# Attention and top-k expert layer on one core: score and AV rounds on 64x64 tiles of TensorE

## The chip, the cores and the metric

The kernel runs on one core of one Trainium2 chip. The metric is the device time of one execution in microseconds (us), the median of several runs. Everything below about time comes from those runs or from one profiled execution.

## What is computed

The input has 8 batches, 12 heads, 448 positions and a head size of 64. First comes attention with normalised q and k, then a layer of 8 experts, each of which takes at most 80 of the 3584 tokens, those with the highest gate weight.

```python
def rmsnorm(x, g):
    rms = np.sqrt(np.mean(x * x, axis=-1, keepdims=True) + 1e-06)
    return x / rms * g
q_n, k_n = (rmsnorm(q, g_q), rmsnorm(k, g_k))
scores = scale * np.matmul(q_n, k_n.transpose(0, 1, 3, 2))
attn = softmax(scores)
x = np.matmul(attn, v)            # -> (3584, 768)
logits = x @ w_gate
expert_idx = np.argmax(logits, axis=1)
gate_w = softmax(logits)[arange(N), expert_idx]
for e in range(E):
    tok_idx = ...                 # tokens of e; over capacity: the 80 of largest gate_w
    h = np.maximum(x[tok_idx] @ w1[e], 0.0)
    out[tok_idx] = gate_w[tok_idx, None] * (h @ w2[e])
```

## The kernel before

**Groups, rounds and slots.** The work of attention is cut into 24 groups (`NG`): a batch has three, of four heads each. The four heads are two pairs, `u` = 0 and 1, and the heads of a pair are `hh` = 0 and 1. A group has seven rounds (`RD`). The loop at the end of the attention part (from L828) goes through slots -10 to 88; in each slot it issues the scores of two rounds (`S2`), the presums and AV of the two rounds before (`A2`), and what tables `begins`, `mid` and `end` have put in that slot. `mid` stands between the scores and AV, `end` behind AV. `NS` = 84 slots have scores, 0 to 83. Instructions stand on each engine in the order in which this loop issues them.

**Layout.** Of the 448 positions, 384 lie on all 128 partitions, three to a partition (`NJ`), and the last 64 (`SR`) on half of them, one pair of heads on each half. So a group has two kinds of rounds. A full round (`score`, L322) takes one pair and 128 keys: two matmuls with 64 rows (the head size) and 128 columns of the array. The round `x == NJ` (L315) takes the last 64 keys of both pairs: four matmuls of 64x64. AV (`av`) mirrors this: L344 with 128 rows (keys) and 64 columns, L337 with 64x64. All are fp32 with 448 moving columns, and each matmul stands in the trace as two instructions.

**Around the rounds.** `load` brings q, k and v into SBUF from SP's queue. `square` (ACT), `rstd` (DVE reduction, then a power on POOL), and `normalise` (POOL; DVE for groups 0 and 1) prepare q and k; `transp` transposes them on TensorE into `tp`, and ACT copies them to `qkT`. The scores land in PSUM (`ps`, two buffers), ACT writes their exponentials to `at` (L324), and DVE adds these up over the rounds (`presum`). When a pair is through, ACT copies its sum over v from PSUM (`uevac`, L367). `xout` transposes that, copies it to `xb` (one buffer) and writes it to HBM, where the experts' tokens are gathered later.

**Gate.** `zl` (L377, L381) multiplies the presums with a selector and the AV sums with the gate's weights, eight matmuls of 32 columns a group, into one PSUM bank of a batch. Then `gate1` (copy), `gate1t` (transposes), `gate1v` (reciprocal and products on DVE), `gate2`, `gate2x`, `gate2b` yield each token's expert and weight. The batches below `NB0` = 4 go through a top-k on DVE in small steps (`rounds`, `numbers`), which `work` hands out by a budget of us a slot. Each later batch is ranked in itself (`rank_in_batch`) and merged into the kept lists (`merge`, five steps); `chain_step` issues one step when its lag is over, twice a slot. What is left is issued behind the last slots, at `s == NS + 2`. The last batch is ranked after the loop (from L870). Then come gathers of tokens and the experts' matmuls (`xpose`, L962 and below).

Of the kernel before, what the change touches and what calls it, by code (L numbers as in the profile page):

```python
# [20 lines left out]
def kernel(  # L21
# [13 lines left out]
    nc = tc.nc  # L35
# [10 lines left out]
    SM = 384  # L46
# [4 lines left out]
    NB = 4 * NJ + 2  # L51
    RD = 2 * NJ + 1
# [12 lines left out]
    NB0 = 4  # L65
# [24 lines left out]

    zsel = cpool.tile([128, NQ, 32], F32, name="zsel")
    nc.vector.memset(zsel[:, :, :], 0.0)
    for i in range(NQ):
        nc.vector.memset(zsel[:, i, 24 + i:25 + i], 1.0)
    wgs = cpool.tile([128, H, 32], F32, name="wgs")
    nc.vector.memset(wgs[:, :, :], 0.0)
    wg_v = moe_w_gate.rearrange("(i c hh d) e -> hh d i c e", hh=2, c=2, d=D)

    def load_wgs():
        for hh in range(2):  # L100
            for i in range(NQ):
                nc.sync.dma_start(
                    out=wgs[hh * D:(hh + 1) * D, 4 * i + hh:4 * i + hh + 3:2, 8 * i:8 * i + 8],
                    in_=wg_v[hh, :, i])
# [12 lines left out]
    for g in range(NB0):  # L117
        nc.gpsimd.memset(offq[32 * g:32 * g + 32, :], float(g * S))
# [18 lines left out]
    nc.gpsimd.iota(rowI[:, 0:NJ], pattern=[[1, NJ]], base=0, channel_multiplier=NJ)  # L137
    nc.gpsimd.iota(rowI[:, NJ:NJ + 1], pattern=[[0, 1]], base=SM, channel_multiplier=1)
# [45 lines left out]
    tpps = ctx.enter_context(tc.tile_pool(name="tp_ps", bufs=1, space=PSUM))  # L184
    zlps = ctx.enter_context(tc.tile_pool(name="zl_ps", bufs=1, space=PSUM))
# [6 lines left out]
    with tc.tile_pool(name="vp", bufs=3) as vpool, \  # L192
         tc.tile_pool(name="attn", bufs=5) as apool, \
# [9 lines left out]
        def load(g, t, src, eng, parts=(0, 1, 2)):  # L203


            b, i = divmod(g, NQ)
            if 0 in parts:
                h0, h1 = (0, 4) if 1 in parts else (0, 2)
            elif 1 in parts:
                h0, h1 = (2, 4)  # L210
            if 0 in parts or 1 in parts:
                eng.dma_start(
                    out=t[:, h0 * NJ:h1 * NJ, :].rearrange("p (h j) d -> p h (j d)", j=NJ),
                    in_=src[b, 4 * i + h0:4 * i + h1, 0:SM].rearrange(
                        "h (p j) d -> p h (j d)", j=NJ))
            if 2 in parts:
                for u in range(2):
                    eng.dma_start(
                        out=t[64 * u:64 * u + 64, 4 * NJ:NB, :],
                        in_=src[b, 4 * i + 2 * u:4 * i + 2 * u + 2, SM:S].rearrange(  # L220
                            "h p d -> p h d"))

        def load_qk(g):
            qk = [qkpool.tile([128, NB, D], F32, tag="qk", name="qk") for _ in range(2)]
            st[g]["qk"] = qk
            if g:
                load(g, qk[0], q, nc.sync)
                load(g, qk[1], k, nc.sync)
            else:
                load(g, qk[0], q, nc.sync, (0, 2))  # L230
                load(g, qk[1], k, nc.scalar, (0, 2))
                load(g, qk[0], q, nc.sync, (1, ))
                load(g, qk[1], k, nc.sync, (1, ))
# [7 lines left out]
        M = 4 * NJ  # L241
        ALLB, HALF = [(0, NB)], ([(0, M // 2), (M, NB)], [(M // 2, M)])

# [7 lines left out]
        def rstd(g, a, parts=ALLB):  # L251
# [8 lines left out]
            for lo, hi in parts:  # L260
                if parts is HALF[0]:
# [6 lines left out]
        def normalise(g, a, parts=ALLB):  # L268
# [3 lines left out]
            eng = nc.vector if g < 2 else nc.gpsimd  # L272
            for lo, hi in parts:
                h0, h1 = lo // NJ, min(hi, M) // NJ
                if h0 < h1:
                    eng.tensor_mul(  # L276
                        qn[:, :M].rearrange("p (j h) d -> p h j d", h=4)[:, h0:h1],
                        qk[:, h0 * NJ:h1 * NJ].rearrange("p (h j) d -> p h j d", j=NJ),
                        rs[:, h0 * NJ:h1 * NJ].rearrange("p (h j) -> p h j", j=NJ)
                        .unsqueeze(3).to_broadcast([128, h1 - h0, NJ, D]))  # L280
                if hi > M:
                    eng.tensor_mul(qn[:, M:], qk[:, M:],
                                   rs[:, M:].unsqueeze(2).to_broadcast([128, 2, D]))

        def transp(g, a, u):
            tp = tpps.tile([128, 512], F32, tag="tp", name="tp")
            qn = st[g]["qn%d" % a]
            for j in range(NJ):
                nc.tensor.transpose(  # L289
                    tp[:, j * 128:(j + 1) * 128],  # L290
                    qn[:, 4 * j + 2 * u:4 * j + 2 * u + 2].rearrange("p h d -> p (h d)"),
                    ident[:, :])
            if u == 0:
                nc.tensor.transpose(tp[:, SM:512],  # L294
                                    qn[:, 4 * NJ:].rearrange("p h d -> p (h d)"), ident[:, :])
                st[g]["T%d" % a] = qktpool.tile([128, 2, S], F32, tag=f"qkT{a}", name="qkT")
            dst = st[g]["T%d" % a]
            parts = [(dst[:, 0, :], tp[:, :S]), (dst[:, 1, SM:], tp[:, S:512])] if u == 0 else \
                [(dst[:, 1, :SM], tp[:, :SM])]
            for o, x in parts:  # L300
                if a == 0:
                    nc.scalar.activation(o, x, AF.Copy, scale=gqk[:, :])  # L302
                else:
                    nc.scalar.copy(o, x)  # L304

        def score(r):
# [3 lines left out]
            if x == NJ:  # L310
                at = apool.tile([128, 2, S], F32, tag="ar", name="ar", bufs=2)
                for u in range(2):
# [740 lines left out]
```

## Time and profile before

| what | us |
|---|---|
| median of 3 runs (lowest, highest) | 532.16 (531.81, 535.04) |
| the profiled execution's own time | 529.9 |
| its span, first to last instruction | 528.2 |

The profile gives, for each engine, when it was busy: PE is TensorE (PEld its weight loads), DVE is VectorE, ACT is ScalarE, POOL is GpSimd, SP issues transfers. A matmul's end is modelled, and matmuls on different tiles overlap, so what a block of them costs is read from the start of one block to the start of the next.

### The profile page before, as it was taken

To read this page: it belongs to the slowest core of one execution; us is meant where nothing else is said; L and a number is where in the kernel's file an instruction comes from. 1 tells how busy PE (TensorE), PEld (TensorE's weight loads), DVE (VectorE), ACT (ScalarE), POOL (GpSimd) and SP (SyncE) were. 2 spreads that over 40 slices of the span, in tenths; PEclk is the share of its full clock that TensorE was granted. 3 is DMA by queue.
4 is the path that set the end of the run, shared out by engine and by line. 5 is a ranking of instruction groups with operands and counts; after the bars stand their busy time and mean duration, and the time that the engine had idled before them with its cause. 6 is when DMAs were issued, how large, how long until landed. Compare 5 with 4: busy or idle time off the path is not lost. (4 is left out here: it accounts for less than half of the span.)

```text
span 528.2 us, 9134 instructions
## 1 busy us (share of the span) xinstructions
PE 495.6 (94%) x3384; PEld 229.2 (43%) x3384; DVE 334.6 (63%) x584; ACT 315.5 (60%) x527; POOL 289.9 (55%) x212
## 2 busy tenths in 40 slices
PE   7599999999999999999999999999999989869595
PEld 7133334333433343334433333334445444568464
DVE  4575365765765658638889969996648555624242
ACT  4576786767767786678676876776666635201100
POOL 3588395883875837828467388474796000121231
PEclk9999999999999999999999999999999989668979
DMA  6469978797969995997789787969495661749931
GB/s 174 116 130 225 246 204 139 216 228 198 222 136 232 221 232 99 228 251 197 134 228 210 208 136 196 252 199 215 140 185 130 128 238 37 238 113 414 366 111 57
DMA packets 107340, 100.74 MB, mean 191 GB/s; under 512 B 28960, under 2 KB 99104, under 8 KB 106016
## 3 DMA queue, kind: packets, MB, share of 16 engines
q1 hardware_dynamic: 90736, 70.76, 45.2%
q0 software_dynamic: 16000, 29.14, 31.4%
q8 instruction: 27, 0.44, 0.4%
q10 hardware_dynamic: 560, 0.26, 0.2%
q14 instruction: 17, 0.14, 0.1%
HBM read 101.12 MB, written 39.91 MB: 267 GB/s over the span
## 5 line engine op out<-in xcount | busy, mean ns | idle before, releaser
L265 POOL TENSOR_TENSOR rs<-ms,nhalf 128x14 f32<-128x14 f32 (+1 forms) x48 | 145.7, 3039 | 130.6 <-DVE ms L258 125.7
L324 ACT ACTIVATE at<-ps 128x896 f32<-128x896 f32 x144 | 125.7, 915 | 32.7 <-PE ps L322 18.9
L322 PE MATMUL ps<-qkT 64*128 64x448 f32 x576 | 131.2, 567 | 0.6 <-ACT qkT L304 0.6
L344 PE MATMUL po<-at,vt 128*64 128x448 f32 x576 | 128.6, 561 | 0.0
L257 DVE TENSOR_REDUCE ms<-sq 128x14 f32<-128x896 f32 (+2 forms) x52 | 52.5, 1010 | 62.6 <-ACT sq L248 62.4
L356 DVE TENSOR_TENSOR sm<-at 128x896 f32<-128x896 f32 x48 | 58.7, 1224 | 26.1 <-ACT at L324 26.1
L276 POOL TENSOR_TENSOR qn<-qk,rs 128x768 f32<-128x768 f32 x44 | 70.1, 1594 | 0.2
L322 PEld LDWEIGHTS ps<-qkT 64*128 64x128 f32 x576 | 48.1, 185 | 49.1 <-issue 33.8
L289 PEld LDWEIGHTS tp<-ident,qn 128*128 128x128 f32 x288 | 30.3, 141 | 64.8 <-issue 54.2
L344 PEld LDWEIGHTS po<-at,vt 128*64 128x64 f32 x576 | 34.2, 137 | 54.1 <-issue 53.3
L363 DVE TENSOR_TENSOR sm<-sm,at 128x896 f32<-128x896 f32 x48 | 54.5, 1136 | 1.5
L289 PE MATMUL tp<-ident,qn 128*128 128x128 f32 x288 | 52.3, 291 | 3.2 <-DVE qn L276 1.7
L304 ACT COPY qkT<-tp 128x448 f32<-128x448 f32 (+2 forms) x72 | 27.2, 413 | 46.6 <-PE tp L294 46.6
L248 ACT ACTIVATE sq<-qk 128x896 f32<-128x896 f32 (+2 forms) x52 | 46.6, 903 | 6.1 <-DMA qk<-in_q_dram 5.9
L302 ACT ACTIVATE qkT<-tp,gqk 128x448 f32<-128x448 f32 (+2 forms) x72 | 34.0, 507 | 15.2 <-PE tp L289 10.8
L994 ACT ACTIVATE h_sb<-ph 128x320 bf16<-128x320 f32 x16 | 7.0, 437 | 56.4 <-PE ph L990 56.0
L680 PEld LDWEIGHTS xp<-ident,us 128*128 128x128 f32 x192 | 20.1, 141 | 32.9 <-issue 31.3
L367 ACT COPY us<-po 128x448 f32<-128x448 f32 x48 | 25.8, 537 | 14.5 <-PE po L337 10.9
L684 ACT COPY xb<-xp 128x512 f32<-128x512 f32 x48 | 28.2, 587 | 8.6 <-DMA xr_scratch<-xb 8.4
L680 PE MATMUL xp<-ident,us 128*128 128x128 f32 x192 | 31.5, 287 | 0.9 <-ACT qkT L302 0.9
L358 DVE TENSOR_TENSOR sm<-sm,ar 64x896 f32<-64x896 f32 x24 | 29.7, 1236 | 0.8
L947 POOL MEMSET xg<- 80x781 f32 x3 | 2.1, 741 | 51.1 <-DMA xr_scratch<-xb 51.1
(186 smaller groups left out, 577.1 us busy)
## 6 DMA issues: line engine op xcount, KB each, us to landing
wb_scratch<-in_moe_w_dram POOLq DMA_DIRECT2D x10, 1536.0 KB, 12.9
w_sb<-wb_scratch SPq DMA_DIRECT2D x10, 1536.0 KB, 12.4
out_dram<-zeros SPq DMA_DIRECT2D x28, 384.0 KB, 3.8
vt<-in_v_dram SPq DMA_DIRECT2D x24, 384.0 KB, 6.7
w_sb<-in_moe_w_dram POOLq DMA_DIRECT2D x6, 1536.0 KB, 12.9
xr_scratch<-xb SPq DMA_DIRECT2D x24, 384.0 KB, 8.2
qk<-in_q_dram SPq DMA_DIRECT2D x23, 384.0 KB, 5.5
qk<-in_k_dram SPq DMA_DIRECT2D x23, 384.0 KB, 5.5
```

What stands on the lines that cost most here:

```text
L248: nc.scalar.activation(st[g]["sq%d" % a][:, lo:hi], st[g]["qk"][a][:, lo:hi], AF.Square)
L257: nc.vector.reduce_sum(out=ms[:, lo:hi], in_=st[g]["sq%d" % a][:, lo:hi], axis=AX.X)
L265: nc.gpsimd.tensor_tensor(rs[:, lo:hi], ms[:, lo:hi], nhalf[:, lo:hi], op=ALU.pow)
L276: eng.tensor_mul(qn[:, :M].rearrange("p (j h) d -> p h j d", h=4)[:, h0:h1], qk[:, h0 * NJ:h1 * NJ].rearrange("p (h j) d -> p h j d", j=NJ ...
L289: nc.tensor.transpose(tp[:, j * 128:(j + 1) * 128], qn[:, 4 * j + 2 * u:4 * j + 2 * u + 2].rearrange("p h d -> p (h d)"), ident[:, :])
L302: nc.scalar.activation(o, x, AF.Copy, scale=gqk[:, :])
L322: nc.tensor.matmul(ps[:, hh, :S], T1[d, u, j * 128:(j + 1) * 128], T0[d, u, :], start=True, stop=True)
L324: nc.scalar.activation(at[:], ps[:, :, :S], AF.Exp)
L344: nc.tensor.matmul(st[g]["po%d" % u][hh * D:(hh + 1) * D, :S], vt[:, (2 * u + hh) * NJ + j, :], at[:, hh, :], start=(x == 0), stop=(x == R ...
L356: nc.vector.tensor_add(sm[:], s["at%d" % (x - 1)][:], s["at%d" % x][:])
L363: nc.vector.tensor_add(sm[:], sm[:], s["at%d" % x][:])
L680: nc.tensor.transpose(xp[:, j * 128:(j + 1) * 128], us[:, c:c + 128], ident[:, :])
```

## The change

All rounds now take 64 keys of all four heads: pair `u` has its keys on partitions 64u to 64u + 63, and each round has four matmuls of 64x64 for the scores and four for AV. To this end q, k and v are loaded with seven consecutive positions (`NX`) to a partition, 1792 bytes in a piece, and one `normalise`, one `uevac` copy and one `presum` serve both pairs. `transp` takes four of seven blocks of 64 positions at a time (`f` = 0), then three. The transposes of `transp` and `xout` all stand in `end`; where a group's last AV round comes first of the two, it is issued before the scores. `zl` is done once a batch with four matmuls a group, `tp` has two buffers, which `zl` and the gate's transposes share. `NB0` is 3, the budget of `work` 1.65, and chain steps come once a slot each. Group 0's prologue is cut by `hh`.

```diff
-    SM = 384
+    NX = S // 64
+    SM = S // 128 * 128
...
-    NB0 = 4
+    NB0 = 3
...
-    tpps = ctx.enter_context(tc.tile_pool(name="tp_ps", bufs=1, space=PSUM))
-    zlps = ctx.enter_context(tc.tile_pool(name="zl_ps", bufs=1, space=PSUM))
+    tpps = ctx.enter_context(tc.tile_pool(name="tp_ps", bufs=2, space=PSUM))
...
+        def load(g, t, src, eng, hhs=slice(0, 2)):
             b, i = divmod(g, NQ)
+            eng.dma_start(
+                out=t[:].rearrange("p (hh x) d -> p hh (x d)", x=NX)[:, hhs],
+                in_=src[b, 4 * i:4 * i + 4].rearrange("(hh u) (p x) d -> (u p) hh (x d)",
+                                                      u=2, x=NX)[:, hhs])
...
-            eng = nc.vector if g < 2 else nc.gpsimd
+            eng = nc.vector if g == 0 and a == 0 or g == 1 else nc.gpsimd
...
+        def transp(g, a, f):
             tp = tpps.tile([128, 512], F32, tag="tp", name="tp")
             qn = st[g]["qn%d" % a]
+            x0, n = (0, 4) if f == 0 else (4, NX - 4)
+            for x in range(n):
                 nc.tensor.transpose(
+                    tp[:, x * 128:(x + 1) * 128],
+                    qn[:, 2 * (x0 + x):2 * (x0 + x) + 2].rearrange("p h d -> p (h d)"),
                     ident[:, :])
...
         def score(r):
...
+            for u in range(2):
                 for hh in range(2):
                     d = slice(hh * D, (hh + 1) * D)
-                    nc.tensor.matmul(ps[:, hh, :S], T1[d, u, j * 128:(j + 1) * 128],
-                                     T0[d, u, :], start=True, stop=True)
+                    nc.tensor.matmul(ps[u * 64:u * 64 + 64, hh, :S],
+                                     T1[d, u, x * 64:(x + 1) * 64], T0[d, u, :],
+                                     start=True, stop=True)
...
         def av(r):
...
+            for u in range(2):
+                p = slice(u * 64, u * 64 + 64)
+                for hh in range(2):
+                    nc.tensor.matmul(po[hh * D:(hh + 1) * D, u, :S],
+                                     vt[p, hh * NX + x, :], at[p, hh, :],
+                                     start=(x == 0), stop=(x == RD - 1))
+            if x == RD - 1:
+                st[g]["us"] = upool.tile([128, 2, S], F32, tag="us", name="us")
+                nc.scalar.copy(st[g]["us"][:], po[:, :, :S])
...
+        def zl(b, groups):
+            if groups[0] == 0:
+                gst[b]["zl"] = tpps.tile([128, 512], F32, tag="tp", name="zl")
             t = gst[b]["zl"]
+            def mm(c, w, x, first, last):
+                nc.tensor.matmul(t[32 * c:32 * c + 32, :S], w, x, start=first, stop=last)
+            for i in groups:
+                s = st[NQ * b + i]
+                c = (2, 3) if i < 2 else (0, 1)
+                for u in range(2):
+                    mm(c[u], wgs[:, 2 * i + u, :], s["us"][:, u, :], i == 0, i == 1)
+                for hh in range(2):
+                    mm(hh, zsel[:, i, :], s["sm"][:, hh, :], i == 0, i == NQ - 1)
...
+                for f in range(2):
+                    at_slot(end, b0 - 4 + 2 * a + f + (g == 0 and a + f == 2), transp, g, a, f)
+            at_slot(end, b0 + 4 + odd, xout, g, 0)
+            at_slot(end, b0 + 5 + odd, xout, g, 1)
...
+            for r in A2:
+                if r % RD == RD - 1 and r < A2[-1]:
+                    av(r)
             for r in S2:
                 score(r)
             for r in A2:
                 presum(r)
             for f, a in mid.pop(s, []):
                 f(*a)
-            if s <= NS and not chain_step(2 * s, "m", merges, False):
-                chain_step(2 * s, "r", ranks, False)
             for r in A2:
-                av(r)
+                if r % RD < RD - 1 or r == A2[-1]:
+                    av(r)
             for f, a in end.pop(s, []):
                 f(*a)
-            if s < NS and not chain_step(2 * s + 1, "r", ranks, False):
-                chain_step(2 * s + 1, "m", merges, False)
+            if s < NS:
+                chain_step(s, "m", merges, False)
+                chain_step(s, "r", ranks, False)
...
-            work(2.15 if s < NS else 9)
+            work(1.65 if s < NS else 9)
```

What this does to the order shows first on PE, in a stretch of about two slots in the early attention phase. `ps` are scores, `po` is AV, `tp` and `xp` are transposes of q or k and of the AV sums, `zl` is the gate. Before:

```order
L322 MATMUL ps<-qkT 128x448 x2
L315 MATMUL ps<-qkT 64x448 x4
L680 MATMUL xp<-ident,us 128x128 x4
L344 MATMUL po<-at,vt 64x448 x4
L377 MATMUL zl<-sm,zsel 32x448 x4
L381 MATMUL zl<-us,wgs 32x448 x4
L289 MATMUL tp<-ident,qn 128x128 x3
L294 MATMUL tp<-ident,qn 128x128
L322 MATMUL ps<-qkT 128x448 x4
L680 MATMUL xp<-ident,us 128x128 x4
L344 MATMUL po<-at,vt 64x448 x2
L337 MATMUL po<-ar,vt 64x448 x4
```

The scores, AV, `zl` and transposes alternate, and in some slots a 64x64 round stands beside a round of another shape. After, on PE, three slots in a row:

```order
L315 MATMUL po<-at,vt 64x448 x4
L300 MATMUL ps<-qkT 64x448 x8
L315 MATMUL po<-at,vt 64x448 x4
L646 MATMUL xp<-ident,us 128x128 x4
L278 MATMUL tp<-ident,qn 128x128 x3
L300 MATMUL ps<-qkT 64x448 x8
L315 MATMUL po<-at,vt 64x448 x8
L646 MATMUL xp<-ident,us 128x128 x4
L278 MATMUL tp<-ident,qn 128x128 x4
```

All matmuls of the rounds of a slot stand together, the transposes behind them, and `zl` is gone from most slots.

The second place is DVE behind the last slots. `keep`, `rank` and `put` are the DVE steps of a merge, `rg<-zt` is the reciprocal of the last batch's gate. Before:

```order
L637 TENSOR_TENSOR keep<-iota,move 80x640
L644 SCALAR_TENSOR_TENSOR rank<-rank,cnt 128x4
L647 TENSOR_TENSOR put<-iota,rank 128x320
L401 RECIPROCAL rg<-zt 128x4x12
L405 TENSOR_TENSOR lx<-zt,rg 128x96 x4
```

One merge's last DVE steps stand ahead of the reciprocal. After, on DVE:

```order
L329 TENSOR_TENSOR sm<-sm,at 128x896 x2
L585 TENSOR_TENSOR ahead<-own,rg 128x320
L589 TENSOR_REDUCE cnt<-ahead 128x4
L602 TENSOR_TENSOR keep<-iota,move 80x640
L609 SCALAR_TENSOR_TENSOR rank<-rank,cnt 128x4
L612 TENSOR_TENSOR put<-iota,rank 128x320
L363 RECIPROCAL rg<-zt 128x4x12
L371 TENSOR_TENSOR lx<-zt,rg 128x4x16 x6
```

A whole merge (`ahead`, `cnt`, `keep`, `rank`, `put`) now stands between the last presums (`sm`) and the reciprocal.

## Rows read from the trace of the kernel before

**Rows 1.** The page, part 1: busy time and share of the span by engine

```profile
PE 495.6 (94%) x3384; PEld 229.2 (43%) x3384; DVE 334.6 (63%) x584; ACT 315.5 (60%) x527; POOL 289.9 (55%) x212
```

**Rows 2.** Stretches: PE, PEld, DVE, ACT, POOL busy, clock, DMA share, GB/s

```profile
250.00:300.00 50.00, 50.00 (x304) 19.99 (x306) 45.28 (x78) 35.41 (x59) 28.70 (x19) 1.00 0.84 190
300.00:350.00 50.00, 50.00 (x304) 19.50 (x298) 44.37 (x96) 35.81 (x57) 35.16 (x25) 1.00 0.90 205
```

**Rows 3.** Timeline of PE, 253 to 267 us: start, us, engine, line, instruction

```profile
253.09 0.96 PE L377 MATMUL zl<-sm,zsel 128*32 128x448 f32 x8
...
254.73 0.55 PE L289 MATMUL tp<-ident,qn 128*128 128x128 f32 x3
...
259.89 1.77 PE L322 MATMUL ps<-qkT 64*128 64x448 f32 x8
261.60 0.55 PE L289 MATMUL tp<-ident,qn 128*128 128x128 f32 x3
262.08 1.72 PE L344 MATMUL po<-at,vt 128*64 128x448 f32 x8
263.73 0.55 PE L289 MATMUL tp<-ident,qn 128*128 128x128 f32 x3
...
264.32 1.02 PE L322 MATMUL ps<-qkT 64*128 64x448 f32 x4
265.27 0.98 PE L315 MATMUL ps<-qkT 64*64 64x448 f32 x8
266.18 0.66 PE L680 MATMUL xp<-ident,us 128*128 128x128 f32 x4
```

**Rows 4.** Groups of weight loads by shape: count, busy us, mean ns, idle before

```profile
L315 PEld LDWEIGHTS ps<-qkT 64*64 64x64 f32 x192 | 5.3, 132 | 14.5 <-issue 7.5 <-ACT qkT L302 4.8 <-ACT at L324 0.7
```

**Rows 5.** DMA: a queue's packets, MB, share; issues, KB each, us to landing

```profile
q1 hardware_dynamic: 90736, 70.76, 45.2%
...
xr_scratch<-xb SPq DMA_DIRECT2D x24, 384.0 KB, 8.2
```

**Rows 6.** Timelines of DVE, POOL and PE in the first 30 us

```profile
10.52 0.16 DVE L86 TENSOR_TENSOR gqk<-gk 128x1 f32<-128x1 f32 x1 [2.15 <-DMA gk<-in_g_k_dram]
...
20.12 1.08 DVE L257 TENSOR_REDUCE ms<-sq 128x14 f32<-128x896 f32 x1
...
20.29 5.13 POOL L265 TENSOR_TENSOR rs<-ms,nhalf 128x14 f32<-128x14 f32 x2 [1.88 <-DVE ms L258]
...
24.24 1.76 PE L315 MATMUL ps<-qkT 64*64 64x448 f32 x4 [4.01 <-ACT qkT L302]
...
29.34 1.77 PE L322 MATMUL ps<-qkT 64*128 64x448 f32 x8
```

**Rows 7.** Timelines of PE, DVE and POOL, 440 to 480 us

```profile
440.68 1.77 PE L322 MATMUL ps<-qkT 64*128 64x448 f32 x8
...
442.97 1.11 PE L612 MATMUL mp<-aval,eqT 8*128 8x80 f32 x8
...
447.73 0.66 PE L680 MATMUL xp<-ident,us 128*128 128x128 f32 x4
...
453.79 0.24 PE L665 MATMUL mp<-ident,ainfo 80*8 80x80 f32 x1 [0.26 <-ACT ainfo L661]
...
444.58 0.49 DVE L620 TENSOR_TENSOR ahead<-own,rg 128x320 bf16<-128x320 f32 x1 [6.20 <-ACT own L616]
...
448.76 0.81 DVE L637 TENSOR_TENSOR keep<-iota,move 80x640 f32<-80x640 f32 x1
...
449.68 0.49 DVE L647 TENSOR_TENSOR put<-iota,rank 128x320 f32<-128x320 f32 x1
...
451.92 0.46 DVE L401 RECIPROCAL rg<-zt 128x48 f32<-128x48 f32 x1 [1.75 <-PE zt L391]
...
464.28 0.16 DVE L939 CAST idxT<-psc 80x8 uint32<-80x8 f32 x1 [1.33 <-PE psc L936]
...
467.46 1.04 POOL L953 DMA_INDIRECT xg<-xr_scratch,idxT  x1 [9.33 <-DMA xr_scratch<-rg]
```

More of the change, by code (lines that the diff above doesn't have):

```diff
@@ L50 @@
     NG = B * NQ
-    NB = 4 * NJ + 2
-    RD = 2 * NJ + 1
+    NB = 2 * NX
+    RD = NX
     DC = DM // 128
@@ L116 @@
     offq = tpool.tile([128, 1], F32, name="offq")
-    for g in range(NB0):
+    for g in range(4):
         nc.gpsimd.memset(offq[32 * g:32 * g + 32, :], float(g * S))
@@ L296, in transp @@
                 st[g]["T%d" % a] = qktpool.tile([128, 2, S], F32, tag=f"qkT{a}", name="qkT")
[L297 to L304, printed above, removed]
+            o = st[g]["T%d" % a][:, :, x0 * 64:(x0 + n) * 64].rearrange(
+                "q u (x p) -> q x u p", p=64)
@@ new lines @@
+            if g:
+                for a in range(2):
+                    at_slot(mid, b0 - 7 + a, square, g, a)
+                    at_slot(end, b0 - 7 + a, rstd, g, a)
+                    at_slot(mid, b0 - 5 + a, normalise, g, a)
+            for a in range(2):
+                for f in range(2):
+                    at_slot(end, b0 - 4 + 2 * a + f + (g == 0 and a + f == 2), transp, g, a, f)
+            at_slot(end, b0 + 4 + odd, xout, g, 0)
+            at_slot(end, b0 + 5 + odd, xout, g, 1)
@@ new lines @@
+        for b in range(B):
+            b0 = (NQ * b + NQ - 1) * RD // 2
+            if b < B - 1:
+                at_slot(end, b0 + 6, zl, b, range(NQ))
+                at_slot(end, b0 + 6, gate1, b)
+            else:
+                at_slot(end, b0 + 3, zl, b, range(NQ - 1))
+                at_slot(end, b0 + 4, zl, b, range(NQ - 1, NQ))
+                at_slot(end, b0 + 4, gate1, b)
+            b0 -= b == B - 1
+            at_slot(end, b0 + 7, gate1t, b)
+            at_slot(mid, b0 + 8, gate1v, b)
+            at_slot(end, b0 + 8, spent, 1.3)
+            if b == B - 1:
+                continue
+            at_slot(mid, b0 + 9, gate2, b)
+            at_slot(end, b0 + 9, gate2x, b)
+            at_slot(end, b0 + 9, spent, 1.5)
+            if b >= NB0:
+                at_slot(mid, b0 + 10, gate2i, b)
+            at_slot(mid, b0 + 10, gate2b, b)
+            at_slot(end, b0 + 10, spent, 1.0)
+            if b == NB0 - 1:
+                at_slot(end, b0 + 10, gate3)
+                at_slot(end, b0 + 10, queue.extend, topk)
+            elif b >= NB0:
+                at_slot(mid, b0 + 10, batch_in, b)
@@ L825 @@
             nc.tensor.matmul(wps[:, i % 2, :ZW], zeros[:, :128], zeros[:, :], start=True, stop=True)
-        for s in range(-10, NS + 5):
+        for s in range(-10, NS + 6):
             for f, a in begins.pop(s, []):
```

254 lines of the change are left out of this document (79 added, 175 removed).

## The prediction

> **What bounds the kernel now.** I read the share of each engine first, then the stretches, then the timeline of TensorE, then the two ends. TensorE is busy 94% of the span [rows 1]. In two stretches of 50 us in the attention phase it is busy for all 50.00 us at a granted clock of 1.00, while DVE is busy for 45.3 and 44.4 us, ACT for 35.4 and 35.8, POOL for 28.7 and 35.2, and the DMA engines for 0.84 and 0.90 of the time [rows 2]. So the slots run one behind the other at the pace of TensorE's own list, and a saving there is a saving in time until another engine takes over. The timeline shows what that list costs, from one start to the next [rows 3]. Two score rounds in one block take 259.89 to 261.60 = 1.71 us, one takes 264.32 to 265.27 = 0.95; the second adds 0.76. One round is two passes (each fp32 matmul stands as two instructions, and those of one pass, on different tiles, run beside each other), so a pass of 448 columns takes 0.38, and I use 0.375. What a block costs above its passes is the price of going from one tile shape to the next: score block 1.71 - 1.50 = 0.21, AV block 262.08 to 263.73 = 1.65, so 0.15; a block of 64x64 tiles 0.91 - 0.75 = 0.16 (265.27 to 266.18); zl 253.09 to 254.73 = 1.64 = 1.50 + 0.14. Three transposes take 0.48 (261.60 to 262.08), four 0.59 (263.73 to 264.32): 0.11 each and 0.15 a block.
>
> **Check of this account on before.** Slot 2 begins at 29.34 [rows 6] and slot 83, the last with scores, at 440.68 [rows 7]: 411.3 us for 81 slots, 5.08 each. Seven slots (two groups) hold 56 passes (21.0), five plain score blocks and two mixed ones that pay 0.20 + 0.16 (1.77), five plain AV blocks and two mixed ones that pay 0.15 + 0.16 (1.37), 44 transposes in 12 blocks (4.84 + 1.80), two zl (3.28) and the gate's transposes (0.3): 34.4 us, 4.91 a slot, 397.6 for 81. The 13.7 left over are the matmuls of the top-k, rank and merge steps.
>
> **The change, part by part.**
> Score and AV. Now every round is four 64x64 matmuls, still two passes, so the 56 passes stay. What goes is the price between shapes: scores and AV of a slot stand back to back on one shape (first order fences) and pay 0.16 once, where before a slot paid about 0.45 and the transposes between them again. The trace holds this shape as one round alone, never several in a row. Bounds for a second round on the same shape: 0.75 (as between the plain rounds), or 0.91 if each round pays its own start. I take 0.75: plain AV blocks and zl (two or four tiles at once) go on at 0.375 a pass.
> [...] The blocks of zl and AV use all 128 rows of the array in every matmul and still go on at 0.375 a pass with their weight loads inside [rows 3]. [...]
> Transposes: the same 14 + 8 a group, now one block a slot at its end: 3.5 blocks a group instead of 6.
> zl: before, eight matmuls for each group (four passes); now four a group, done once a batch. Groups 0 and 1 use four column tiles at once (two passes each), group 2 has only two tiles for four matmuls (four passes): 8 x 0.375 + 0.14 = 3.14 a batch instead of 3 x 1.64 = 4.92.
> Sum of a group (3.5 slots): 28 passes 10.50, 3.5 blocks 0.56, 22 transposes 2.42, their blocks 0.53, zl 1.05, gate's transposes 0.15 = 15.21, so 4.35 a slot and 352 for 81. With four in-batch ranks instead of three and the merges that still fit I put 15 for the small matmuls: 367 instead of 411.3, that is -44. Below, I bound it by 360 (if the small ones share blocks with the transposes) and 406 (each round pays 0.16: three more in a slot, +0.48 x 81 = +39).
> DVE: its presums, reductions and gates stay (six full adds a group, as before). It ran 45.3/50 of 5.08 = 4.60 a slot in the top-k stretch, with a budget of 2.15 for extra work; the budget is now 1.65, so 4.10 to 4.17, of a slot of 4.53: 0.92 where it was 0.906 with TensorE never idle. ACT: 35.8/50 x 5.08 = 3.64 before; six copies of transposes become four, two of AV become one: at most 3.64 of 4.53, 0.80. POOL: at most 3.57 of 4.53. None of these takes over by its sum; but rows in order on each engine make some waits, which I put at 4 us over all (bounds 0 and 17, below).
> DMA: 0.84 to 0.90 of 5.08 is 4.27 to 4.57 us a slot, the one that comes closest. The loads of q, k and v go from 512 pieces of 768 bytes and 256 of 256 bytes a tile to 256 pieces of 1792 bytes; 72 tiles make 55,296 of the 90,736 packets of queue q1, whose packets take 45.2% of 528.2 x 16 = 42 ns each [rows 5]. If their time goes by bytes nothing is won and the slot is held at 4.57, +3 us over 81 slots; if by packets, up to 2/3 of their share goes. I take that DMA does not bind, which costs 0 to 3 us.
> The start. Now all of q and the first four key blocks, and the first transposes of group 1, come before the first score, so it begins later; but the stall of slot 1, whose scores waited for the second half of the heads until 24.24 [rows 6], goes. The first transposes of group 1 need its square, its reduction on DVE (1.08, queued behind the gains that came at 10.52) and POOL's power (5.13 for two) and then DVE's product: about 16 [rows 6]. So I put the first score at 16.6, slot 1 at 19 and slot 2 at 24 instead of 29.34: -5. Bounds: 0 (a wait in the same place) and -7.
> The end. From the start of slot 83 to the end of the last AV: 447.73 - 440.68 = 7.05 now; after, the slot's own block 3.16, zl of two groups 1.64, some small matmuls 0.35 and the last AV block 1.66 = 6.8. Then a loss: only three batches go through the first top-k now (NB0 = 3), the merges come one step a slot, and that of batch 6 is left whole for behind the last slot. On DVE its steps stand ahead of the last gate's reciprocal (second order fences). That reciprocal began at 451.92, 4.2 after the last AV. After, it waits for the merge of batch 5 to end (453.79 to about 454.2, 6.5 after) and then for one more chain: matmuls 1.11, copy 0.4, two DVE steps of 0.49 (the second put like the first), matmuls 0.3, ACT 0.3, keep, rank and put 0.81 + 0.15 + 0.49, and some 1.0 of hand-overs: 5 to 6. It starts 12.2 after instead of 4.2: +8. But the first gather (467.46) stood 3.0 behind the index (464.28 + 0.16) for the gate's rows behind 3 MB of weights; 8 us later these have landed: -3. Net +5, bounds 0 and +10 [rows 7].
>
> **Sum.** -5 (start) - 44 (slots) + 0 + 5 (end) + 4 (waits) = -40 to -41. The profiled execution's own time is 529.9 (span 528.2 and 1.7 around it), so 489 for one like it; the median of the runs lies 2.3 above, so 491.5.
>
> **The rivals.**
> A. Another engine takes the slots of the top-k stretch: DVE at 0.92 with presums that wait for ACT and free the buffers late, or DMA. If these some 35 slots stay at 5.0, +0.47 x 35 = 17: 508. For: 0.92 leaves little. Against: 0.906 cost nothing before.
> B. ACT is held by the copy of transposed rows: its tile xb has one buffer, the write to HBM takes a median 8.2 us to land [rows 5], and the gap between groups shrinks from two slots of 5.08 to two of 4.53 (9.1). One us a group reaching TensorE is 24: 515.
> C. Each round on the new shape pays its own start: +39, which leaves 530: no change.
> [...]
>
> **How the numbers follow.** Forecast 0.75, A 0.12, B 0.06, C 0.03, D 0.04. The forecast's own range is 478 to 503 (start +-3, slots 360 to 372, end +-5). To leave no more than 2 in 10 outside, the range reaches over A and touches B: 475 to 514. A measurement of this kernel tells about 1% from no change, 5 us. Faster by over 1%: forecast, A, B, 0.93; within: C, 0.03; slower: D, 0.04.
>
> **What would show it.** Right: a score and an AV block in a row without a step, eight passes in 3.16; TensorE busy near all of the time in the attention phase; slot starts 4.4 to 4.6 apart; slot 2 near 24; a full merge between the last AV and the last gate's reciprocal. Wrong: idle TensorE that ends on ACT or DVE in the slots (A, B), passes further apart than 0.38 (C, D), a last stretch behind the last AV that is not near 85.5 us.

## The result: 4.3% faster, a little over half of what was forecast

| | before | after |
|---|---|---|
| median of the runs of this comparison | 533.6 us (4 runs, 531.81 to 539.29) | 511.49 us (4 runs, 509.49 to 512.96) |
| ratio, 95% interval | 1 | 0.9566 [0.9483, 0.9648] |
| profiled execution | 529.9 us, span 528.2 | 512.96 us, span 511.3 |
| granted clock, mean of the span | 0.965 | 0.942 |
| start of slot 2 | 29.34 us | 28.64 us |
| slots 2 to 83 (81 slots) | 411.3 us | 388.8 us |
| start of slot 83 to end of last AV | 7.05 us | 6.8 us |
| end of last AV to end of the span | 80.5 us | 87.1 us |

A later set of runs of the changed kernel gave 512.67 us and 0.9600 [0.9525, 0.9675]. The forecast was 491.5 with 478 to 503 as its own range. That range missed; the wide one, 475 to 514, holds the result only because it had been drawn to reach over rival A. The span is 24.0 us above the 24 + 371 + 6.8 + 85.5 = 487.3 that the forecast's terms make: 4.6 at the start, 17.8 in the slots (388.8 against 367 and 4 of waits), 0 from slot 83 to the last AV, 1.6 at the end. The lines that the slots and the last AV are read from:

```profile
28.64 1.74 PE L300 MATMUL ps<-qkT 64*64 64x448 f32 x16
...
417.41 1.74 PE L300 MATMUL ps<-qkT 64*64 64x448 f32 x16
...
422.46 1.73 PE L315 MATMUL po<-at,vt 64*64 64x448 f32 x16
```

The page's shares of the changed kernel, to be read beside [rows 1] (busy us, share of the span, instructions):

```profile
PE 465.7 (91%) x4409; PEld 236.4 (46%) x4409; DVE 367.2 (72%) x620; ACT 308.2 (60%) x459; POOL 277.2 (54%) x167
```

The stretches that answer to [rows 2] (us, busy time and instructions of PE, PEld, DVE, ACT, POOL, then the granted clock, DMA share, GB/s):

```profile
200.00:250.00 50.00, 47.46 (x438) 20.45 (x430) 48.07 (x81) 36.37 (x51) 27.89 (x14) 0.97 0.85 206
250.00:300.00 50.00, 45.57 (x414) 19.43 (x410) 43.10 (x81) 33.21 (x48) 31.46 (x19) 0.97 0.84 197
300.00:350.00 50.00, 47.22 (x444) 21.28 (x436) 40.88 (x80) 33.99 (x52) 34.24 (x22) 0.93 0.79 189
```

TensorE was busy for all of 50.00 us in two of these stretches before, at a clock of 1.00. Now it is idle for 2.5 to 4.4 us in each, the mean clock of each is below 1.00, and DVE is busy for 48.07 of the first 50 us.

Where nothing waits, the slots are what the forecast said. TensorE's timeline of one of them, up to the start of the next (start us, us, engine, line, instruction):

```profile
112.70 1.74 PE L300 MATMUL ps<-qkT 64*64 64x448 f32 x16
114.26 1.68 PE L315 MATMUL po<-at,vt 64*64 64x448 f32 x16
115.87 0.66 PE L646 MATMUL xp<-ident,us 128*128 128x128 f32 x4
116.37 0.60 PE L278 MATMUL tp<-ident,qn 128*128 128x128 f32 x4
116.90 1.73 PE L300 MATMUL ps<-qkT 64*64 64x448 f32 x16
```

From the start of the scores to that of the transposes is 3.17 us, for eight passes and one change of shape; the forecast had 3.16. The slot with eight transposes takes 4.20 us.

The idle time stands in the chain of waits of TensorE, 25 to 425 us (who waited for whom, us in total, times, longest):

```profile
PE tp L278 <- DVE lx L371: 6.4, 4, 2.4
PE mp L594 <- DVE ahead L585: 2.6, 1, 2.6
PE zl L338 <- ACT qkT L290: 1.7, 1, 1.7
PE tp L278 <- POOL qn L266: 1.6, 2, 1.1
PE sp L440 <- DVE sc L418: 1.6, 1, 1.6
```

Of the 15.5 us of such waits, in 14 places, 10.6 end on DVE, 1.6 on POOL's products and the rest on ACT. The price is more than that, since the granted clock fell from 1.00 to 0.50 at some of them. Four stretches:

```profile
226.00:229.00 3.00, 0.81 (x8) 0.42 (x5) 2.96 (x11) 1.88 (x3) 1.35 (x1) 1.00 0.00 0
229.80:233.10 3.30, 3.30 (x24) 1.15 (x20) 3.20 (x6) 1.82 (x3) 2.88 (x1) 0.50 0.02 5
332.20:339.00 6.80, 6.63 (x52) 3.06 (x55) 5.11 (x12) 2.56 (x4) 6.28 (x5) 0.50 0.64 91
366.30:373.10 6.80, 6.26 (x56) 2.67 (x56) 6.63 (x13) 2.77 (x5) 2.39 (x1) 0.50 1.10 244
```

TensorE worked for 0.81 of the 3 us before 229.0, and then ran at a granted clock of 0.50 (half clock below) from 229.76 to 233.17. Four such stretches inside the slots, 20.5 us together (the fourth, near 270.7, is not among the lines), cost about 10 us of work, an estimate that takes half of the time: a score block that lasted 1.74 us at 1.00 (from 112.70) lasted 3.27 at 0.50 (from 20.19). Before, there was one, of 3.4 us. Taking both off the 388.8 leaves about 363, a little under the 367 of the forecast. So the account of shapes and passes holds, and what failed is the term for waits.

Why is DVE late? Its timeline in one such place, with POOL's beside it:

```profile
266.45 4.18 POOL L266 TENSOR_TENSOR qn<-qk,rs 128x896 f32<-128x896 f32 x2
...
267.72 1.36 DVE L327 TENSOR_TENSOR sm<-at 128x896 f32<-128x896 f32 x1
268.19 0.42 PEld L278 LDWEIGHTS tp<-ident,qn 128*128 128x128 f32 x4 [1.33 <-POOL qn L266]
268.19 0.66 PE L278 MATMUL tp<-ident,qn 128*128 128x128 f32 x4 [1.09 <-POOL qn L266]
...
269.12 2.46 DVE L329 TENSOR_TENSOR sm<-sm,at 128x896 f32<-128x896 f32 x1
```

An add that runs beside none of POOL's products takes 1.09 us (103 of them). The 41 beside a product take 2.04 in the mean, and the 41 products beside an add 2.01, where the three of this size that meet none take 1.68. The two wait for each other: of the 27 adds that start during a product, 24 end 0.95 us behind that product's end, however long it runs; the other three start in its last 0.06 us. A product that starts during an add and outlasts it ends 1.54 to 1.67 us behind the add's end. Over all 144 adds the excess above 1.085 us is 39.5 us; in the kernel before it was 15.2. The groups of adds before (first two lines) and after, with POOL's products after (line, operation, count, busy us, mean ns, idle before):

```profile
L356 DVE TENSOR_TENSOR sm<-at 128x896 f32<-128x896 f32 x48 | 58.7, 1224 | 26.1 <-ACT at L324 26.1
L363 DVE TENSOR_TENSOR sm<-sm,at 128x896 f32<-128x896 f32 x48 | 54.5, 1136 | 1.5
...
L329 DVE TENSOR_TENSOR sm<-sm,at 128x896 f32<-128x896 f32 x120 | 169.5, 1413 | 6.9 <-ACT at L303 0.9
L266 POOL TENSOR_TENSOR qn<-qk,rs 128x896 f32<-128x896 f32 (+1 forms) x46 | 88.8, 1946 | 4.8 <-DVE rs L254 4.6
```

POOL's power (3.1 us in the mean) does nothing of this: 62 adds run beside it alone and keep their 1.09 us.

### The profile page after: what moved, and what is told of

The parts are those of the page before. It is cut to its first block, busy times and chain, and to the rows that moved or that the text cites. A ratio compares the mean times of both kernels' runs of the same rounds, so it can differ in the third digit from the quotient of the medians.

```text
span 511.3 us, 10958 instructions
## 1 busy us (share of the span) xinstructions
PE 465.7 (91%) x4409; PEld 236.4 (46%) x4409; DVE 367.2 (72%) x620; ACT 308.2 (60%) x459; POOL 277.2 (54%) x167
## 3 DMA queue, kind: packets, MB, share of 16 engines
q1 hardware_dynamic: 52208, 70.55, 43.8%
## 5 line engine op out<-in xcount | busy, mean ns | idle before, releaser
L256 POOL TENSOR_TENSOR rs<-ms,nhalf 128x14 f32<-128x14 f32 x46 | 142.5, 3100 | 116.4 <-DVE ms L249 109.6
L329 DVE TENSOR_TENSOR sm<-sm,at 128x896 f32<-128x896 f32 x120 | 169.5, 1413 | 6.9 <-ACT at L303 0.9
L300 PE MATMUL ps<-qkT 64*64 64x448 f32 x1344 | 151.6, 567 | 0.6 <-ACT eqT L572 0.4
L315 PE MATMUL po<-at,vt 64*64 64x448 f32 x1344 | 147.0, 547 | 0.0
L266 POOL TENSOR_TENSOR qn<-qk,rs 128x896 f32<-128x896 f32 (+1 forms) x46 | 88.8, 1946 | 4.8 <-DVE rs L254 4.6
L315 PEld LDWEIGHTS po<-at,vt 64*64 64x64 f32 x1344 | 51.0, 136 | 73.2 <-issue 68.8
L248 DVE TENSOR_REDUCE ms<-sq 128x14 f32<-128x896 f32 (+1 forms) x50 | 52.2, 1043 | 42.1 <-ACT sq L239 42.0
L300 PEld LDWEIGHTS ps<-qkT 64*64 64x64 f32 x1344 | 44.8, 136 | 61.6 <-issue 43.7
L278 PE MATMUL tp<-ident,qn 128*128 128x128 f32 x336 | 54.6, 286 | 13.5 <-DVE lx L371 6.4
L278 PEld LDWEIGHTS tp<-ident,qn 128*128 128x128 f32 x336 | 38.2, 144 | 41.7 <-issue 16.8
L239 ACT ACTIVATE sq<-qk 128x896 f32<-128x896 f32 (+1 forms) x50 | 46.2, 926 | 1.6 <-DMA qk<-in_q_dram 1.6
L290 ACT COPY qkT<-tp 128x512 f32<-128x512 f32 (+1 forms) x48 | 25.7, 536 | 11.6 <-PE tp L278 11.6
L988 POOL DMA_INDIRECT out_dram<-yo,idxT x8 | 7.6, 945 | 35.8 <-DVE yo L983 13.4
L320 ACT COPY us<-po 128x896 f32<-128x896 f32 x24 | 21.7, 906 | 7.5 <-PE po L315 7.4
L327 DVE TENSOR_TENSOR sm<-at 128x896 f32<-128x896 f32 x24 | 26.3, 1094 | 0.0
```

The costliest lines, as they stand in the source:

```text
L239: nc.scalar.activation(st[g]["sq%d" % a][:, lo:hi], st[g]["qk"][a][:, lo:hi], AF.Square)
L248: nc.vector.reduce_sum(out=ms[:, lo:hi], in_=st[g]["sq%d" % a][:, lo:hi], axis=AX.X)
L256: nc.gpsimd.tensor_tensor(rs[:, lo:hi], ms[:, lo:hi], nhalf[:, lo:hi], op=ALU.pow)
L266: eng.tensor_mul(qn[:].rearrange("p (x hh) d -> p hh x d", hh=2)[:, h0:h1], qk[:, lo:hi].rearrange("p (hh x) d -> p hh x d", x=NX), rs[:, ...
L278: nc.tensor.transpose(tp[:, x * 128:(x + 1) * 128], qn[:, 2 * (x0 + x):2 * (x0 + x) + 2].rearrange("p h d -> p (h d)"), ident[:, :])
L300: nc.tensor.matmul(ps[u * 64:u * 64 + 64, hh, :S], T1[d, u, x * 64:(x + 1) * 64], T0[d, u, :], start=True, stop=True)
```

## The experiments

The kernel before ran beside each of these sets, at 531.5 to 532.0 us. "Slots" below is the time from slot 2 to slot 83 in the profiled execution, "tail" that from the end of the last AV to the end. In the six profiles whose tails hold after's program it varies between 85.8 and 88.1. The changed kernel itself ran only in the first set and beside e10 and e11, so elsewhere a step of a few us between two kernels is read from the ratios and the profiles, not from medians alone.

The slots of each kernel can be taken apart as those of after were above: TensorE's idle time (here with the gaps too short to be listed as waits), half of its busy time at half clock, and the rest, which is its list of work.

| profile | slots | idle | lost at half clock | the rest |
|---|---|---|---|---|
| before | 411.3 | 3.1 | 1.7 | 406.5 |
| after | 388.8 | 15.8 | 9.9 | 363.1 |
| after once more | 387.3 | 16.8 | 6.8 | 363.8 |
| e3 | 375.3 | 11.6 | 0 | 363.7 |
| e4 | 394.5 | 11.7 | 7.3 | 375.4 |
| e5 | 401.2 | 20.8 | 10.2 | 370.2 |
| e8 | 392.2 | 18.3 | 8.3 | 365.7 |
| e10 | 380.6 | 13.4 | 4.4 | 362.9 |
| e10 once more | 379.1 | 12.5 | 3.4 | 363.2 |
| e11 | 385.1 | 15.8 | 6.3 | 363.0 |

The rest is 363 to 364 us in after, e3, e10 and e11, whose lists are alike, whatever the waits are. The loss at half clock differs between two executions of one kernel by 1 to 3 us, and e14, whose slots are issued as e10's are, has none.

**e1: free the transposes' buffer.** The gate's transposes zt hold one of two `tp` buffers until DVE has read them; here ACT copies them away (and POOL fills the padded columns again).

```diff
-            gst[b]["zt"] = zt
+            nc.scalar.copy(zsb[:, :], zt[:, :])
+            gst[b]["zt"] = zsb
...
+            if b < B - 1:
+                nc.gpsimd.memset(zsb[:, S:], 1.0)
```

> Edit: behind the gate's transposes ACT copies their PSUM bank to SBUF, and the gate's products on DVE read the copy, so the bank no longer waits for DVE. Theory 1 (the changed kernel's TensorE waits because the gate's transposes now hold one of the two transpose banks until DVE gets to the gate, and each such wait is followed by a stretch at half clock): the four waits of 2.2, 1.7, 2.4 and 0.2 us on the gate's products go, and with them the half-clock stretches near 230 and 332 us (3.4 and 6.8 us at half rate, 5.1 lost): 8 to 11 us less than the changed kernel's 511.5, so 500 to 504. Rival (DVE is simply late in the top-k stretch, and another wait takes the place): 509 to 513.

512.09 us, 0.9645 [0.9576, 0.9714]; slots 386.7: the rival's time. The waits that it was made for are gone, and others took their place, as the same view shows:

```profile
PE tp L278 <- POOL qn L266: 6.7, 5, 2.3
PE ps L300 <- ACT row L526: 2.2, 1, 2.2
PE sp L443 <- DVE sc L421: 1.8, 1, 1.8
```

So the buffer is where the lateness showed, not what made it.

**e2: the start.** Group 1's first transposes stand behind the first scores.

```diff
-                    at_slot(end, b0 - 4 + 2 * a + f + (g == 0 and a + f == 2), transp, g, a, f)
+                    at_slot(end, b0 - 4 + 2 * a + f + (g == 0 and a + f == 2 or g == 1 and a + f == 0), transp, g, a, f)
```

> Edit: the first transposes of group 1 stand behind the first scores instead of ahead of them. Theory: the first score waited for group 1's normalise (TensorE idle 4.0 us ahead of 19.2), and the clock fell to half at 18.1 for 6.8 us because of it; without it the first score starts near 16 and slot 2 near 24 instead of 28.6: 3 to 5 us less, 506 to 508. Rival (the next thing, the transposes of group 1 behind the first scores, waits as long): 510 to 513.

508.29 us, 0.9592 [0.9536, 0.9648], just above the theory's 506 to 508. First score 16.01 instead of 20.19, slot 2 at 24.28 instead of 28.64, and no stretch at half clock there. By the ratio alone e2 can't be told from after; the gain of 4.4 us is read at slot 2. The forecast had put slot 2 at 24; what kept it at 28.64 was this wait in the changed kernel:

```profile
19.18 1.08 PE L278 MATMUL tp<-ident,qn 128*128 128x128 f32 x4 [3.98 <-DVE qn L266]
20.19 3.27 PE L300 MATMUL ps<-qkT 64*64 64x448 f32 x16
```

**e3: no products.** From `g` = 4 on the normalisation's products are left out, and the transposes read the tiles of earlier groups again: a part of the computation is missing.

```diff
+            if g >= 4:
+                st[g]["qn%d" % a] = st[g - 2]["qn%d" % a]
+                return
```

> Edit: from group 4 on the products of q and k with their reciprocal norms on POOL are left out (the transposes read the normalised tiles of groups 2 and 3 again); all else runs. Theory 2 (DVE is late because its adds run beside POOL's products: 38 adds that overlap one take 2.12 us in the mean, the others 1.09): all adds take 1.09, 35 us of DVE's time go, TensorE's waits on DVE (gate products, merge) and the half-clock stretches behind them shrink: 10 to 17 us less than 511.5, 494 to 501. If the place of the waits alone counts (theory 1 without 2): the adds get faster, but 508 to 512.

500.6 us, 0.9438 [0.9392, 0.9483]: 11 us less than after. The adds' excess falls from 39.5 to 3.1 us, slots to 375.3, and no stretch between slots 2 and 83 is at half clock:

```profile
200.00:250.00 50.00, 46.89 (x445) 20.58 (x441) 42.24 (x80) 36.11 (x52) 18.49 (x8) 1.00 0.84 211
```

Of the idle time 11.6 us are left, so that of the 13.5 us that the slots lose some 10 are the clock's. The run takes away three things at once, though: the collision, 42 us of DVE's time, and the transposes' wait for their own group's product. e8 takes away the collision alone.

**e4: the price of a block.** The transposes of the output rows stand between scores and AV again, so that in their slots the 64x64 tiles are left and taken up once more.

```diff
-            at_slot(end, b0 + 4 + odd, xout, g, 0)
-            at_slot(end, b0 + 5 + odd, xout, g, 1)
+            at_slot(mid, b0 + 5 + odd, xout, g, 0)
+            at_slot(mid, b0 + 6 + odd, xout, g, 1)
```

> Edit: the transposes of the AV sums go back between the scores and AV of a slot (one slot later than now), which undoes one part of the change. By the account of blocks each of 48 such places splits the slot's 64x64 block (0.16 us) and makes a transpose block more (0.15): 48 x 0.31 = 15 us more than 511.5, 524 to 528. Rival (such steps are hidden by waits that are there anyway): 509 to 516.

524.81 us, 0.9872 [0.981, 0.9935]: 13 us more than after; slots 394.5, tail 92.6. The time is the theory's 524 to 528, but in part by luck. TensorE's list in the slots gets 12.3 us longer, 0.26 to 0.27 for each of the 46 to 48 places that lie there, where 0.31 was expected; its idle time and its loss at half clock are 6.7 lower together, so the slots grow by only 5.7. The tail adds 5.5, which the account of blocks does not have; why, the run doesn't show.

**e5: the chain of rank and merge steps as before,** twice a slot, once in its middle, with the lags of before.

```diff
...
-            if s < NS:
-                chain_step(s, "m", merges, False)
-                chain_step(s, "r", ranks, False)
+            if s <= NS and not chain_step(2 * s, "m", merges, False):
+                chain_step(2 * s, "r", ranks, False)
...
+            if s < NS and not chain_step(2 * s + 1, "r", ranks, False):
+                chain_step(2 * s + 1, "m", merges, False)
```

> The merge and rank steps are taken twice in a slot again, with the lags of the kernel before; all else as in the changed kernel. Theory (the tail is longer because the whole merge of the last batch stands ahead of the last gate's reciprocal): from the last AV product's end to the kernel's end 80 to 82 us in place of 87.2, and the reciprocal 4 to 7 us behind that product in place of 14.2; the slots stay within 3 us of 388.8; time 504 to 508. Rival 1 (the tail's length comes from the gate and the gathers and not from the merge): tail 86 to 88, time 510 to 513. Rival 2 (steps in the middle of a slot break the block on 64x64 tiles, and the mode is paid again): tail 80 to 82, slots 5 to 10 us longer, time 509 to 515.

517.71 us, 0.9728 [0.9636, 0.9821], above all three ranges; rival 2 is nearest. Both halves of the question got an answer. The tail is 78.3 instead of 87.1, and the last gate's reciprocal starts 4.7 us behind the last AV. The slots are 401.2, 12.4 longer, 7.1 of it in TensorE's list and 5.0 in idle time: the steps in the middle of a slot break the block, and 11 of TensorE's 24 idle moments there stand before such a step (most of 0.3 us, waiting for ACT's exponentials). From slot 83 to the last AV it takes 2.3 us more as well. The change's choice of one step at a slot's end pays more than it costs.

**e7: the product in two halves.**

```diff
-        def normalise(g, a, parts=ALLB):
+        def normalise(g, a, parts=None):
+            if parts is None:
+                parts = HALF[0] + HALF[1] if g >= 2 else ALLB
```

> GpSimd's product of a group from the third on is issued as two of 448 elements in place of one of 896. Theory (an add beside a product waits until that whole instruction ends): an add can slip in behind the first half, so the excess of the adds over 1.085 us falls from 39.5 us to 15 to 25, the slots get 4 to 9 us shorter, time 502 to 508. [...]

516.7 us, 0.974 [0.9666, 0.9815]. The excess falls only to 30.7 us (47 adds beside a product, 1.73 each), and POOL pays 19.9 us more. The products come later and TensorE waits for them in eight places instead of two. The theory's 502 to 508 is missed. Its mechanism holds, since an add that starts during a half again ends 0.95 us behind that half's end; but the second half then waits for the add, and the next add for it. So splitting does not help.

**e8: the products on DVE.**

```diff
-            eng = nc.vector if g == 0 and a == 0 or g == 1 else nc.gpsimd
+            eng = nc.gpsimd if g == 0 and a == 1 else nc.vector
```

> The products of the normalisation go to VectorE from the third group on. Theory 1 (VectorE's lateness is the lock with GpSimd's products): adds at 1.1 us, excess under 6 us; 44 products of about 1.11 us add 49 us to VectorE, so its busy time goes from 367 to about 378 us; the transposes wait less for qn; since in the top-k stretch VectorE stays near its end (48 of 50 us: less 5 for the excess, more 7 for the products), time 503 to 510. Theory 2 (VectorE's own count is what binds, however it comes about): VectorE over 49 of 50 us in the stretch from 200 to 250, TensorE's idle time there grows from 3.8 us to over 6, time 513 to 520.

514.02 us, 0.9685 [0.9606, 0.9763], slots 392.2. DVE's costliest groups in this kernel (line, operation, count, busy us, mean ns, idle before):

```profile
L329 DVE TENSOR_TENSOR sm<-sm,at 128x896 f32<-128x896 f32 x120 | 130.5, 1088 | 7.0 <-ACT at L303 2.7
...
L266 DVE TENSOR_TENSOR qn<-qk,rs 128x896 f32<-128x896 f32 (+1 forms) x48 | 51.1, 1064 | 2.8 <-POOL rs L256 2.8
```

The collision is gone altogether (excess 0.2 us), DVE's busy time is 364.2 as before the edit (367.2), and so is the result: no gain. The time is theory 2's, but neither theory fits whole: from 200 to 250 DVE is busy for 46.60 us, not 49, and TensorE is idle for 4.0, not over 6. So taking the collision away is not enough by itself. Whether DVE's time per slot is what binds, as e3 against e8 suggests, e10 answers.

**e10 and e11: slack.** e10 takes e2, e8 and e1 together and issues square, root and product of each group from the fourth on one slot earlier; e11 is the same with the products left on POOL.

```diff
+                    e = g > 2
-                    at_slot(mid, b0 - 7 + a, square, g, a)
-                    at_slot(end, b0 - 7 + a, rstd, g, a)
-                    at_slot(mid, b0 - 5 + a, normalise, g, a)
+                    at_slot(mid, b0 - 7 - e + a, square, g, a)
+                    at_slot(end, b0 - 7 - e + a, rstd, g, a)
+                    at_slot(mid, b0 - 5 - e + a, normalise, g, a)
```

> Four edits together: the first transposes of group 1 stand behind the first scores (as in e2_prologue), the products are VectorE's (as in e8_dve_norm), ScalarE's copy frees the gate's transposes (as in e1_zt_copy), and square, root and product of a group from the fourth on are issued one slot earlier. Theory (TensorE's idle moments in the slots come from VectorE running late within its 74%, and a slot of slack takes them away): waits for lx and qn gone, no stretch at half clock between slots 2 and 75, slots 2 to 83 372 to 380 us as with the products left out (375.3), time 493 to 499. Rival (VectorE is full in the top-k stretch, and each wait that goes comes back at the next operand of the same engine): slots 2 to 83 385 to 392, time 505 to 512.

> As e10_dve_copy_lead, but with the products still on GpSimd. Theory (slack is what is missing, and the lock between GpSimd's products and VectorE's adds costs only where VectorE is late): adds still 1.35 us in the mean, but waits for lx and qn gone; slots 375 to 383, time 496 to 503. Rival (the lock fills VectorE in the top-k stretch and slack is eaten up there): slots 384 to 390, time 504 to 511.

> The changed kernel itself once more, unedited, on the same chip as the two above, to place them: 509 to 514 by its first runs.

On one chip: e10 501.71 us, 0.9414 [0.9353, 0.9474]; e11 504.48, 0.9446 [0.9372, 0.952]; after 512.67, 0.9600. So e10 takes 11 us off the changed kernel, of which the start is 3. Its slots are 380.6 (e11 385.1, after 387.3 in this set), a little over the theory's 372 to 380. Its time lies between the theory's 493 to 499 and the rival's 505 to 512, and two stretches at half clock are left between slots 2 and 75, where the theory had none. Its longest waits from 25 to 405 us are these:

```profile
PE mp L597 <- DVE ahead L588: 3.7, 1, 3.7
PE zl L338 <- ACT xb L654: 2.3, 3, 1.6
PE zl L338 <- ACT qkT L290: 2.3, 1, 2.3
PE ps L300 <- ACT row L526: 1.3, 1, 1.3
```

No lx and no qn is left, with DVE as busy as it was (363.5 us). In the stretch from 200 to 250 it is even fuller than in after, and TensorE is idle less and at full clock:

```profile
200.00:250.00 50.00, 48.06 (x454) 20.66 (x450) 48.53 (x88) 37.84 (x54) 19.65 (x10) 1.00 0.86 206
```

So DVE's time per slot is not by itself what costs; late operands fit better, though no run parts the lead from the other edits. And the waits did not go away as a whole: 13.1 us are left where after has 15.5, 8.7 of them ending on ACT and 4.4 on DVE (a merge step, and `sc`). Of the 6.7 us that e10's slots gain on those of after in this set, 3.4 are idle time, 2.4 the clock. e11 came out on its rival's numbers (slots 384 to 390, time 504 to 511), though its waits for lx are gone and those for qn down to 0.4 us. Against e2 (508.29) it gains 4 us by the medians and 8 by the ratios, but only 2 in the profiled slots; its profile is of the slowest of its four runs. e10 and e11 differ by 2.8 us, which their intervals don't tell apart.

**e14: the last gate first.** On top of e10, DVE's part of the last gate goes ahead of the merge of batch 6.

```diff
-            if s == NS + 2:
+            if s == NS + 5:
+                gate2(B - 1)
+                gate2x(B - 1)
                 h = 9999
...
-    gate2(b)
-    gate2x(b)
```

> e10_dve_copy_lead, with VectorE's part of the last gate (reciprocal, products, sum, maximum) issued ahead of the merge of batch 6 in place of behind it; the rest of the tail in its old order. Theory of the forecast (the reciprocal's wait of 8 to 10 us is what lengthens the tail): reciprocal at 4 to 6 us behind the last AV product, VectorE's idle 9.2 us gone, the tail 5 to 8 us shorter, time 493 to 497. Rival (the merge's own chain on TensorE, which the last stage needs for aval, ends at the same time whatever VectorE does, and the reciprocal only stood in its shadow): tail 0 to 3 us shorter, time 498 to 501.5.

> e10_dve_copy_lead once more, unedited, on the same chip as e14_gate_first, to place it: 500 to 503.

e14 502.27 us, 0.9438 [0.9386, 0.949]; e10 once more 500.42, 0.9403 [0.9345, 0.9461]. DVE and the merge's matmuls on TensorE in e14:

```profile
418.23 0.45 DVE L364 RECIPROCAL rg<-zsb 128x48 f32<-128x48 f32 x1 [3.67 <-ACT zsb L355]
...
425.61 0.49 DVE L588 TENSOR_TENSOR ahead<-own,rg 128x320 bf16<-128x320 f32 x1 [4.39 <-ACT own L584]
...
421.37 0.24 PE L633 MATMUL mp<-ident,ainfo 80*8 80x80 f32 x1 [2.20 <-ACT ainfo L629]
...
434.06 1.14 PE L867 MATMUL psa<-aval,eqT 8*128 8x80 f32 x4
```

The reciprocal starts 5.9 us behind the last AV (412.33) instead of 13 to 14, and the tail is 88.8, longer than either range had it: nothing won. The merge's chain (ainfo, aval) has to end before TensorE's matmul on aval at 434.06. That is 21.7 us behind the last AV, against 19.4 in e10's second profile: ACT's copy of ainfo came 2 us later here, behind the gate's exponential. So the run shows that a sooner reciprocal is not enough; it does not show what a sooner one would bring with the merge's chain left in its place.

## Why the prediction came out as it did

**Score and AV on one shape, the blocks, zl: right.** Eight passes and one change of shape take 3.17 us (3.16 forecast), the slots without waits and at full clock 363 (367 forecast). The 4 us between have a likely source: of the 13.7 us that the check on before left to the small matmuls, 3.1 were idle time and 1.7 the loss at half clock. Rival C (each round pays its own start) would have made the eight passes 3.64 us. Rival D (slower, 0.04) fell: a weight load of 0.132 us [rows 4] on top of each pass would have made steps of 0.51, by estimate; the steps are 0.38, with four 64x64 tiles in use, and no run shows loads that come on top. That a change of shape has about the price put on it, e4 bears out (0.26 to 0.27 for 0.31 a place).

**Waits, "4 us over all (bounds 0 and 17)": this is the step that failed.** They cost 15.5 us idle and about 10 at half clock, over the upper bound; what the clock loses behind a wait the term did not have at all. Two things were missed. The forecast gave DVE 4.10 to 4.17 us a slot, from its busy time before, and did not ask what its adds cost beside the products: 39.5 us of excess instead of 15.2. In slots 41 to 51 (199 to 251 us) DVE took 4.56 us a slot, of 4.74. Why the excess was less before no run shows; e7, with the products in halves, still has 30.7. And the forecast took a share of 0.92 as enough because 0.906 had been enough before. But now operands come late (lx, whose reading frees the transposes' buffer, qn, a merge's `ahead`), TensorE's whole list stops there, and at some of these stops the clock fell to 0.50. Three runs bear on it: with less DVE time (and no products) the kernel gains 11 us; with the same DVE time and no collision nothing; with the same DVE time, a slot of slack and the buffer freed 7 to 8, beside the start's 3. That a full DVE alone does not cost is shown by e10; that a slot of slack is the remedy is likely, not shown, since e10 makes four edits at once.

**Rival A** had the place and the price (508 against 511.49) at a chance of 0.12. Of its two candidates it was DVE and not DMA, and not a steady 5.0 a slot but single waits of 0.2 to 2.6 us and the half clock behind some of them; so the near hit in time is in part luck. **Rival B**: TensorE's waits for xb are 1.0 us from 25 to 425; it fell.

**The start, "-5": came as -0.7.** "About 16" for group 1's first product was too early: DVE had it at 17.92 to 19.03, and TensorE stood for 3.98 us and ran at half clock from 18.1 to 25.0. With that order undone (e2) the forecast's own 24 is met.

**The end, "+5": +6.6, right in size; its reason holds half.** The merge of batch 6 does stand before the reciprocal, which starts 14.1 us behind the last AV (12.2 forecast), as DVE's timeline shows:

```profile
435.63 0.49 DVE L585 TENSOR_TENSOR ahead<-own,rg 128x320 bf16<-128x320 f32 x1 [9.22 <-ACT own L581]
...
437.93 0.49 DVE L612 TENSOR_TENSOR put<-iota,rank 128x320 f32<-128x320 f32 x1
438.33 0.45 DVE L363 RECIPROCAL rg<-zt 128x48 f32<-128x48 f32 x1
...
452.25 0.16 DVE L912 CAST idxT<-psc 80x8 uint32<-80x8 f32 x1 [1.33 <-PE psc L909]
```

But the reciprocal's place is not all that costs: e14 moved it and won nothing. The merge's whole chain behind the last slot is the likelier cost: e5, which has it done earlier, has a tail 8.8 us shorter, 2.3 of which it pays between slot 83 and the last AV. e5 does not part this from the clock, since TensorE is at half clock for 23.9 us of its tail and for 32.3 of after's. Of the gather's 3 us 2.2 came: it starts (453.25) 0.8 behind the index's end.

**DMA: does not bind, as taken.** No wait of TensorE from 25 to 425 us ends on it. Its queue shows which of the two prices was true:

```profile
q1 hardware_dynamic: 52208, 70.55, 43.8%
```

42% fewer packets than in [rows 5] take 43.8% of 511.3 instead of 45.2% of 528.2: 224 us for 239. The time went by bytes far more than by packets.

**What is left open:** why the tail of e4 is longer, and which of e10's three edits beside the start brings how much. The copy alone (e1) and the products on DVE alone (e8) brought nothing; the lead alone was not run. How much of after's lost clock belongs to which wait is open too, since it differs between two executions.

## To carry to other kernels

When one engine's list gets shorter by a tenth, give each engine behind it its time per step in the new arrangement, with what it loses beside its neighbours, and look for the operands that have no step of slack: here they stopped TensorE long before DVE's share reached 1. A share of 0.72 of the span, 0.96 in one stretch of 50 us, went with some 25 us of waits and lost clock, while e10 with 0.97 in that stretch was at full clock there. And a wait that can be seen is often not its own cause: freeing the buffer alone (e1), removing the collision alone (e8) and moving the late instruction alone (e14) each brought nothing.

## What had not been expected

The kernel e10, with the same work as the changed one, runs at 500.4 to 501.7 us, 0.94 of the time before; it is the fastest here that computes all.

With four 64x64 tiles in use the eight passes of a block went on at 0.38 us each, weight loads included: in the slot that starts at 112.70 the loads of three passes in a row start at 113.13, 113.51 and 113.89 us and take 0.15 each, while TensorE goes on with its matmuls.

In the slots of the changed kernel, four idle stretches of TensorE of 1.7 to 2.6 us came with 3.4 or 6.8 us at half clock, which began in the idle stretch or when TensorE was busy again (229.8 to 233.1 above): that added up to 1.7 or 3.4 us to the wait, by the same estimate of one half. Not each did this: behind the idle 1.65 us that ended at 284.94 the clock stayed at 1.00.

A VectorE add that started during one of GpSimd's products waited for the end of that whole instruction, at 896 elements as at 448 (e7): 24 of 27 in the changed kernel ended 0.95 us behind it.
